# Scores of the 128-key tile in the burst and banks of the 384-key tile, and a VectorE write ahead of each burst

## The chip, the cores and the metric

The kernel runs on one core of one Trainium2 chip. The metric is device time in microseconds of one execution; the time before is the median of three runs, 1286.41 us (1285.4 to 1286.81). The profile is that of one further execution.

## The reference

Attention over 8 batches and 8 heads with 576 positions and 64 columns per head, masked in blocks of 64 (a query sees the keys of its own block and of those before it), and behind it a feed-forward network with a rational activation:

```python
scores = (1 / sqrt(64)) * q @ k^T                     # 8 x 8 heads, 576 x 576, float32
scores = where(block_i >= block_j, scores, -1e9)      # blocks of 64 positions
scores = scores - max(scores)
attn = exp(scores); attn = attn / (sum(attn) + 1e-9)
x = (attn @ v)                                        # put together to 4608 x 512
h = x @ w_in                                          # 512 -> 2048
P = a0 + a1*h + a2*h^2 + a3*h^3
Q = 1 + |b0|*|h| + |b1|*h^2
out = (P / (Q + 1e-6)) @ w_out                        # 2048 -> 512
```

## The kernel before

Attention runs over 32 pairs of heads (`NP`), two heads at a time: head 0 lies in partitions 0 to 63 of the prepared q and k, head 1 in 64 to 127. Matrix products are made of float32r parts: q and k are each split into a high and a low part, and three products (high-high, high-low, low-high) are added in PSUM.

A pair's queries are cut into five tiles, worked in the order `TILES = (4, 3, 2, 0, 1)`. Tile i below 4 has 128 queries and sees 128*(i+1) keys, so tile 3 is the 512-key tile, tile 2 the 384-key tile, tile 0 the 128-key tile, tile 1 the 256-key tile; tile 4 has the last 64 queries of both heads and 576 keys. Each tile is two steps (j = 0 and 1), so a pair has ten steps, and `attn_steps` hands out a list of what each step does: scores now, the exponential (`expo`) one step later, the transposes (`transp`) six steps later, and the products with v (`pv`) after that. `prep` of the next pair (transposes and splits of q and k) is put between.

For tiles 0 to 3 the scores of both heads are made at j = 0 in one burst. It takes two PSUM banks from a pool of five (`ps_a`, tag "a"), one for each head, and issues four matmuls for each head, in turn head 1 and head 0: first the mask (`MASKS[0]`; L504), a product of a constant row and column that puts a large negative number into the 64 columns that the first 64 queries must not see, and then the three score products (L507). These matmuls use 64 rows of the array each, and so two of them, one for each head, can run beside one another; nearly all other matmuls use all 128 rows. The helper `behind` fixes the order of a burst's matmuls among themselves, without a wait. At each step VectorE takes the maximum of one head's scores (`reduce_max`, L518; L514 for tile 4), and ACT makes the exponential from the bank with the maximum as bias (L529), which frees the bank.

The FFN runs over units of hidden columns: `first` (L210) makes h in one bank of its own, ACT, POOL and VectorE make the activation from it, and `second` (L277) multiplies with w_out. Attention steps from the fifth pair on emit a planned number of FFN half-steps, so FFN matmuls are the filler of the attention part; what is left of the FFN follows when attention is over.

The order of instructions on each engine is not written by hand: a scheduler plays the program through with a cost model when the kernel is built, and gives each engine its queue in the order in which things become ready there. On the chip each engine works its queue in that order and waits on semaphores. So a matmul whose bank is late in the plan can have other matmuls put ahead of it.

Names used below: PE is TensorE's matmul, PEld its weight load, DVE is VectorE, ACT ScalarE, POOL GpSimd. L567 are the transposes of the probabilities, whose results ACT copies (L580) and VectorE splits (L581); L594, L617 and L633 are products with v; L491 the scores of tile 4; L416 the transposes of `prep`.

Of the kernel before, what the change touches and what calls it, by code (L numbers as in the profile page):

```python
# [8 lines left out]
F32 = mybir.dt.float32  # L9
# [3 lines left out]
AF = mybir.ActivationFunctionType  # L13
ALU = mybir.AluOpType
AX = mybir.AxisListType
# [10 lines left out]
LEND = 4  # L26
RL = 3
C0 = 0
RW = 4
EV = 6  # L30
DP = 12
# [27 lines left out]
MASKS = ((None, None), (0, 0), (0, 1), (1, 0))  # L59
# [6 lines left out]
def attn_ffn_kernel(  # L66
# [11 lines left out]
    nc = tc.nc  # L78
# [30 lines left out]
    class Weights:  # L109
# [22 lines left out]
        def convert(self):  # L132
            last = []
            for key in self.places:
# [8 lines left out]
                                        in_=src.bitcast(I32).rearrange("(d p) f -> p d f", p=128))  # L143
                if there and len(last) >= RW:
                    tc.add_manual_dep(got.ins, last[-RW].ins.name,
                                      mybir.DependencyInfo(mybir.DependencyClass.Sync, mybir.DependencyReason.DATA),
# [26 lines left out]
    class Ffn:  # L173
# [8 lines left out]
        def load(self, ph, c):  # L182
            n = CTS[ph]
            nd = 512 // n
            self.x[ph, c] = []
            for i in range(4 // nd):

                pool = self.pools[-1] if ph and (4 * c + i) % 6 < 3 else ffn
                x = pool.tile([128, nd, 2, n], F32R, name=f"x{ph}_{c}_{i}", tag="x", bufs=XB)
                t0 = c * n  # L190
                while t0 < (c + 1) * n:
                    b = t0 // S
                    t1 = min((c + 1) * n, (b + 1) * S)
                    for d in range(nd):
                        nc.sync.dma_start(out=x[:, d, :, t0 - c * n:t1 - c * n].bitcast(F32),
                                          in_=xscr[b][:, nd * i + d, :, t0 - b * S:t1 - b * S])
                    t0 = t1
                self.x[ph, c] += [x[:, d] for d in range(nd)]
# [135 lines left out]
    with ExitStack() as actx:  # L334
        ps_a = actx.enter_context(tc.tile_pool(name="ps_a", bufs=5, space=PSUM))
# [9 lines left out]
        mrow = apers.tile([128, 128], F32R, name="mrow")  # L345
        mcol = apers.tile([128, 64], F32R, name="mcol")
# [55 lines left out]
        def behind(ins, first):  # L402
            tc.add_manual_dep(ins.ins, first.ins.name,
                              mybir.DependencyInfo(mybir.DependencyClass.NoSync, mybir.DependencyReason.DATA),
                              reason="order")
# [74 lines left out]
        def scores(p, d, j):  # L480
            s = st_[p]
            if j == 0:
                s[d] = tuple(att.tile([128, 2], F32, name=f"{n}{p}_{d}", tag=n, bufs=4) for n in ("nm", "sm"))
            nm, sm = s[d]
            i = TILES[d]
            q, k = s["q"], s["k"]
            if i == 4:
                c0, w = 288 * j, 288
                ps = ps_a.tile([128, 512], F32, name=f"s{p}_{d}_{j}", tag="a")
                for n, (x, y) in enumerate(((0, 0), (0, 1), (1, 0))):  # L490
                    nc.tensor.matmul(ps[:, :w], lhsT=qtl[p % 2][:, x], rhs=k[:, y, c0:c0 + w],  # L491
                                     start=(n == 0), stop=(n == 2))
                s[d, j] = ps
            else:
                w = 128 * (i + 1)
                if j == 0:
                    for h in range(2):
                        s[d, h] = ps_a.tile([128, 512], F32, name=f"s{p}_{d}_{h}", tag="a")
                    prev = None
                    for n, (x, y) in enumerate(MASKS):  # L500
                        for h in (1, 0):
                            hs = slice(64 * h, 64 * h + 64)
                            if x is None:
                                mm = nc.tensor.matmul(s[d, h][:, w - 64:w], lhsT=mrow[hs], rhs=mcol[hs],  # L504
                                                      start=(n == 0), stop=(n == 3), skip_group_check=(n == 0))
                            else:
                                mm = nc.tensor.matmul(s[d, h][:, :w], lhsT=q[hs, x, 128 * i:128 * i + 128],  # L507
                                                      rhs=k[hs, y, 0:w], start=(n == 0), stop=(n == 3),
                                                      skip_group_check=(MASKS[0][0] is None))
                            if prev is not None:  # L510
                                behind(mm, prev)
                            prev = mm
            if i == 4 and j == 1:
                nc.vector.tensor_tensor_reduce(out=trash, in0=s[d, j][:, :w], in1=zero.to_broadcast([128, 288]),  # L514
                                               scale=-1.0, scalar=nm[:, 0:1], op0=ALU.add, op1=ALU.min,
                                               accum_out=nm[:, 0:1])
            else:
                nc.vector.reduce_max(out=nm[:, j:j + 1], in_=s[d, j][:, :w], axis=AX.X, negate=True)  # L518

        def expo(p, d, j):  # L520
            s = st_[p]
            nm, sm = s[d]
            i = TILES[d]
            if i == 4 and j == 0:
                return
            for j2 in (0, 1) if i == 4 else (j,):
                n, w = (0, 288) if i == 4 else (j2, 128 * (i + 1))
                dst = pts[4][:, 288 * j2:288 * j2 + 288] if i == 4 else pts[i][:, j2]
                nc.scalar.activation(out=dst, in_=s.pop((d, j2))[:, :w], func=AF.Exp,  # L529
                                     bias=nm[:, n:n + 1], scale=1.0, accum_out=sm[:, j2:j2 + 1])  # L530
            if j == 0:
                return
            rc = att.tile([128, 2], F32, name=f"rc{p}_{d}", tag="rc", bufs=4)
            n = 1 if i == 4 else 2
            if i == 4:
                nc.gpsimd.tensor_tensor(out=sm[:, 0:1], in0=sm[:, 0:1], in1=sm[:, 1:2], op=ALU.add)
            nc.gpsimd.tensor_scalar_add(rc[:, :n], sm[:, :n], 1e-9)
            nc.vector.reciprocal(rc[:, :n], rc[:, :n])  # L538
            for j2 in range(n):
                x = pts[4][:, 0:S] if i == 4 else pts[i][:, j2]  # L540
                nc.gpsimd.tensor_scalar(out=x, in0=x, scalar1=rc[:, j2:j2 + 1], scalar2=1.0,  # L541
                                        op0=ALU.mult, op1=ALU.mult)
# [102 lines left out]
        def attn_steps():  # L645
# [8 lines left out]
            for k in range(len(items) + ALAG2 + ALAG3 + 8):  # L654
                for x in [x for x in todo if x[0] == k]:
                    todo.remove(x)
                    x[1](*x[2])
                if k < len(items):
                    p, d, j = items[k]
                    if (d, j) == (0, 0):  # L660
                        if p + 1 < NV:
                            o0, o1, o2 = OFFS
                            at(k + o0, load, p + 1)
                            at(k + o1, prep, p + 1, 0)
                            at(k + o2, prep, p + 1, 1)
                    at(k + ALAG2, expo, p, d, j)
                    if j == 1:
                        at(k + TLAG, transp, p, d)
                        if d == 4:
                            at(k + TLAG + 1, pv, p, 0)  # L670
                            at(k + TLAG + 2, pv, p, 1)
                            if p + 1 < NV:
                                at(k + TLAG + 2, vprep, p + 1)
                    scores(p, d, j)
                yield k
# [4 lines left out]
        load(0)  # L680
        for _ in range(C0):
            next(wsteps)
# [18 lines left out]
        NWA, NWB = 2 * NFA, 2 * NFB  # L701
        wdone = C0
        WSTEPS = [0] * C0 + [(W0 * (i + 1)) // 4 for i in range(4 - C0)] + [WA + WD * i // 4 for i in range(NWA - 4)]

# [56 lines left out]
```

## Time and profile before

| | |
|---|---|
| median of three runs | 1286.41 us |
| the profiled execution | 1287.04 us |
| its span from first to last instruction | 1285.3 us |
| mean granted TensorE clock | 0.998 |
| PE busy | 1255.0 us, 7644 matmuls |
| ACT busy | 925.3 us |
| DVE busy | 904.0 us |
| POOL busy | 880.5 us |
| DMA, mean | 120 GB/s |

The busy time of PE is a sum over spans whose ends are modelled: a matmul's row runs on while the next has begun. How fast work goes is therefore read from the distance between starts. In a timeline a row gives start, length, engine, line, operation, tiles and count; rows of one line that follow each other are merged. In a list of waits a row names who waited for whom, with the total in microseconds, the number of times and the longest. In the groups of instructions the numbers behind the bar are busy microseconds and the mean nanoseconds of one, and behind the next bar the idle time of the engine just before them and what ended it. The shares of the chain are shares of the time of the chain of work that ended last.

### The profile page before, as it was taken

To read this page: it belongs to the slowest core of one execution; us is meant where nothing else is said; L and a number is where in the kernel's file an instruction comes from. 1 tells how busy PE (TensorE), PEld (TensorE's weight loads), DVE (VectorE), ACT (ScalarE), POOL (GpSimd) and SP (SyncE) were. 2 spreads that over 40 slices of the span, in tenths; PEclk is the share of its full clock that TensorE was granted. 3 is DMA by queue.
4 is the path that set the end of the run, shared out by engine and by line. 5 is a ranking of instruction groups with operands and counts; after the bars stand their busy time and mean duration, and the time that the engine had idled before them with its cause. 6 is when DMAs were issued, how large, how long until landed. Compare 5 with 4: busy or idle time off the path is not lost.

```text
span 1285.3 us, 22748 instructions
## 1 busy us (share of the span) xinstructions
PE 1255.0 (98%) x7644; PEld 1059.5 (82%) x7644; DVE 904.0 (70%) x1703; ACT 925.3 (72%) x2047; POOL 880.5 (69%) x1041
## 2 busy tenths in 40 slices
PE   7989999999999999999999999999999999999997
PEld 5667888888888888888888888888998888888886
DVE  5767678777777777777767676754666767666675
ACT  5878777788678788777878787866766565555553
POOL 4656677777777878777767676766777666666564
PEclk9999999999999999999999999999999999999999
DMA  8772253445444354443432432356111433333423
GB/s 223 210 213 74 71 170 89 131 109 144 107 121 123 114 140 112 131 126 82 135 91 74 114 93 67 89 175 232 50 49 50 131 98 125 125 129 130 155 75 107
DMA packets 206516, 153.81 MB, mean 120 GB/s; under 512 B 137792, under 2 KB 170560, under 8 KB 206400
## 3 DMA queue, kind: packets, MB, share of 16 engines
q1 hardware_dynamic: 203920, 151.77, 40.5%
q8 instruction: 61, 1.00, 0.3%
q10 hardware_dynamic: 2416, 0.59, 0.2%
q14 instruction: 55, 0.45, 0.1%
q0 software_dynamic: 64, 0.00, 0.0%
HBM read 98.57 MB, written 44.04 MB: 111 GB/s over the span
## 4 chain that ended last, share of the span: by engine, by line
PE 82%; ACT 7%; DVE 4%; DMA 3%; POOL 3%; issue 1%; SPq 0%; ACTq 0%; POOLq 0%; DVEq 0%
PE h L210 30%; PE o L277 28%; PE o L633 6%; PE t L567 5%; PE s L507 4%; PE s L504 3%; ACT p L529 2%; PE tp L416 2%; PE s L491 1%; PE o L594 1%; DMA x<-xscr 1%; PE o L617 1%; DMA xscr<-xl 1%; POOL u L244 1%; ACT s L219 1%
## 5 line engine op out<-in xcount | busy, mean ns | idle before, releaser
L210 PE MATMUL h<-x,wpi 128*128 128x256 f32 (+1 forms) x2808 | 462.8, 312 | 3.1 <-DMA x<-xscr 1.7
L210 PEld LDWEIGHTS h<-x,wpi 128*128 128x128 f32 x2808 | 396.4, 190 | 40.6 <-issue 4.0
L277 PE MATMUL o<-wpo,gh 128*128 128x512 f32 x1152 | 351.0, 397 | 1.3 <-ACT os L287 1.3
L277 PEld LDWEIGHTS o<-wpo,gh 128*128 128x128 f32 x1152 | 211.1, 188 | 43.7 <-ACT os L287 1.8
L277 PE MATMUL o<-wpo,gl 128*128 128x512 f32 x576 | 213.8, 401 | 1.2 <-POOL gl L256 1.1
L224 POOL TENSOR_TENSOR u<-v,u 128x512 f32<-128x512 f32 x144 | 186.7, 1297 | 29.7 <-ACT v L220 24.6
L541 POOL TENSOR_SCALAR p<-p,rc 128x128 f32<-128x128 f32 (+4 forms) x288 | 169.2, 599 | 48.0 <-DVE rc L538 40.3
L529 ACT ACTIVATE p<-s,nm 128x288 f32<-128x288 f32 (+4 forms) x320 | 167.8, 533 | 45.1 <-DVE nm L518 39.9
L225 DVE TENSOR_TENSOR s<-s,h 128x512 f32<-128x512 f32 x144 | 98.4, 683 | 110.4 <-ACT s L219 56.7
L244 POOL TENSOR_TENSOR u<-s,u 128x512 f32<-128x512 f32 x90 | 116.7, 1297 | 72.1 <-DVE u L242 58.1
L232 ACT ACTIVATE v<-u,qcb 128x512 f32<-128x512 f32 x144 | 105.1, 730 | 74.7 <-POOL u L224 74.3
L217 ACT ACTIVATE u<-h 128x512 f32<-128x512 f32 x144 | 86.0, 597 | 93.7 <-PE h L210 87.9
L518 DVE TENSOR_REDUCE nm<-s 128x1 f32<-128x128 f32 (+4 forms) x288 | 128.5, 477 | 23.8 <-PE s L507 16.2
L567 PE MATMUL t<-ident,p 128*128 128x128 f32 x800 | 126.5, 281 | 0.9 <-POOL u L224 0.4
L581 DVE TENSOR_TENSOR ptrl<-t,ptrh 128x512 fp32r<-128x512 f32 (+1 forms) x182 | 111.6, 627 | 18.9 <-ACT ptrh L580 17.4
L277 PEld LDWEIGHTS o<-wpo,gl 128*128 128x128 f32 x576 | 104.3, 189 | 23.5 <-POOL gl L256 3.3
L256 POOL TENSOR_TENSOR gl<-u,v 128x512 fp32r<-128x512 f32 x90 | 118.6, 1317 | 3.4
L259 POOL TENSOR_TENSOR gl<-s,gh 128x512 fp32r<-128x512 f32 x54 | 69.9, 1294 | 62.9 <-ACT gh L258 62.9
L567 PEld LDWEIGHTS t<-ident,p 128*128 128x128 f32 x800 | 92.8, 142 | 23.1 <-issue 8.1
L580 ACT CAST ptrh<-t 128x512 fp32r<-128x512 f32 (+1 forms) x182 | 95.7, 545 | 18.8 <-PE t L567 18.2
L226 DVE SCALAR_TENSOR_TENSOR s<-s,coef,h 128x512 f32<-128x512 f32 x144 | 107.2, 744 | 2.9
L507 PE MATMUL s<-k,q 64*128 64x512 f32 (+3 forms) x768 | 103.5, 351 | 0.0
(109 smaller groups left out, 2105.6 us busy)
## 6 DMA issues: line engine op xcount, KB each, us to landing
x<-xscr SPq DMA_DIRECT2D x56, 256.0 KB, 3.8
xscr<-xl SPq DMA_DIRECT2D x32, 288.0 KB, 2.4
pscr<-os SPq DMA_DIRECT2D x18, 512.0 KB, 3.1
pt<-pscr SPq DMA_DIRECT2D x36, 256.0 KB, 4.3
out_dram<-os SPq DMA_DIRECT2D x36, 256.0 KB, 3.5
qr<-in_q_dram SPq DMA_DIRECT2D x64, 128.0 KB, 2.8
kr<-in_k_dram SPq DMA_DIRECT2D x62, 128.0 KB, 2.5
xt<-xh SPq DMA_DIRECT2D x52, 144.0 KB, 2.3
```

The source lines that it names most:

```text
L210: nc.tensor.matmul(h[:, j, :], lhsT=self.w[ph].win(f, dc, y), rhs=xs[dc][:, hl, :], start=(dc == 0 and i == 0), stop=(dc == 3 and i == 2))
L224: nc.gpsimd.tensor_tensor(out=ut, in0=vt, in1=ut, op=ALU.mult)
L226: nc.vector.scalar_tensor_tensor(out=st, in0=st, scalar=a1, in1=hf, op0=ALU.add if ph == 0 else ALU.subtract, op1=ALU.mult)
L244: nc.gpsimd.tensor_tensor(out=ut, in0=st, in1=ut, op=ALU.subtract)
L256: nc.gpsimd.tensor_tensor(out=gl, in0=ut, in1=vt, op=ALU.mult)
L277: nc.tensor.matmul(self.o[m], lhsT=g[:, j, ms], rhs=self.w[ph].wout(f, y), start=(u == 0 and j == 0 and i == 0), stop=(u == nu - 1 and j = ...
L507: mm = nc.tensor.matmul(s[d, h][:, :w], lhsT=q[hs, x, 128 * i:128 * i + 128], rhs=k[hs, y, 0:w], start=(n == 0), stop=(n == 3), skip_group ...
L518: nc.vector.reduce_max(out=nm[:, j:j + 1], in_=s[d, j][:, :w], axis=AX.X, negate=True)
L529: nc.scalar.activation(out=dst, in_=s.pop((d, j2))[:, :w], func=AF.Exp, bias=nm[:, n:n + 1], scale=1.0, accum_out=sm[:, j2:j2 + 1])
L541: nc.gpsimd.tensor_scalar(out=x, in0=x, scalar1=rc[:, j2:j2 + 1], scalar2=1.0, op0=ALU.mult, op1=ALU.mult)
L567: nc.tensor.transpose(ps[:, 128 * x:128 * x + 128], src[:, 128 * kb:128 * kb + 128], ident)
L581: nc.vector.tensor_tensor(out=dl, in0=src, in1=dh.bitcast(F32), op=ALU.subtract)
```

## The change

- The 128-key tile (i = 0) no longer takes banks and no longer has a burst of its own. Its scores are put into columns 384 to 511 of the 384-key tile's two banks, by three products for each head inside that tile's burst. One mask matmul for each head covers both tiles: its right-hand side is repeated, and it writes two groups of 64 columns (columns 320 to 383 and 448 to 511).
- Maximum and exponential of the 128-key tile stay at their own steps and read columns 384 to 511.
- Ahead of each burst (tiles 3, 2 and 1, with `TP = 0` for all pairs) VectorE writes 0.0 into column 0 of head 0's bank, which is the bank that the burst's second matmul writes. The burst's first matmul, which writes head 1's bank, waits for this write.

```diff
-                if j == 0:
-                    for h in range(2):
-                        s[d, h] = ps_a.tile([128, 512], F32, name=f"s{p}_{d}_{h}", tag="a")
+                if j == 0 and i:
+                    both = [ps_a.tile([128, 512], F32, name=f"s{p}_{d}_{h}", tag="a") for h in range(2)]
+                    parts = ((2, 0), (0, 384)) if i == 2 else ((i, 0),)
+                    for t, c in parts:
+                        for h in range(2):
+                            s["s", t, h] = both[h][:, c:c + 128 * (t + 1)]
                     prev = None
+                    held = nc.vector.memset(both[0][:, 0:1], 0.0) if p >= TP else None
                     for n, (x, y) in enumerate(MASKS):
-                        for h in (1, 0):
-                            hs = slice(64 * h, 64 * h + 64)
-                            if x is None:
-                                mm = nc.tensor.matmul(s[d, h][:, w - 64:w], lhsT=mrow[hs], rhs=mcol[hs],
-                                                      start=(n == 0), stop=(n == 3), skip_group_check=(n == 0))
-                            else:
-                                mm = nc.tensor.matmul(s[d, h][:, :w], lhsT=q[hs, x, 128 * i:128 * i + 128],
-                                                      rhs=k[hs, y, 0:w], start=(n == 0), stop=(n == 3),
-                                                      skip_group_check=(MASKS[0][0] is None))
-                            if prev is not None:
-                                behind(mm, prev)
-                            prev = mm
+                        for t, c in parts[:1] if x is None else parts:
+                            for h in (1, 0):
+                                hs = slice(64 * h, 64 * h + 64)
+                                if x is None:
+                                    m = both[h].rearrange("p (s t) -> p s t", t=64)[:, 2 * i + 1:8:2][:, :len(parts)]
+                                    mm = nc.tensor.matmul(m, lhsT=mrow[hs], start=True, stop=False, skip_group_check=True,
+                                                          rhs=mcol[hs].unsqueeze(1).to_broadcast([64, len(parts), 64]))
+                                else:
+                                    mm = nc.tensor.matmul(s["s", t, h], lhsT=q[hs, x, 128 * t:128 * t + 128],
+                                                          rhs=k[hs, y, 0:128 * (t + 1)], start=False, stop=(n == 3),
+                                                          skip_group_check=True)
+                                if prev is not None:
+                                    behind(mm, prev)
+                                elif held is not None:
+                                    tc.add_manual_dep(mm.ins, held.ins.name,
+                                                      mybir.DependencyInfo(mybir.DependencyClass.Sync, mybir.DependencyReason.DATA),
+                                                      reason="order")
+                                prev = mm
...
-                nc.vector.reduce_max(out=nm[:, j:j + 1], in_=s[d, j][:, :w], axis=AX.X, negate=True)
+                nc.vector.reduce_max(out=nm[:, j:j + 1], in_=s[d, j][:, :w] if i == 4 else s["s", i, j],
+                                     axis=AX.X, negate=True)
...
-                nc.scalar.activation(out=dst, in_=s.pop((d, j2))[:, :w], func=AF.Exp,
+                nc.scalar.activation(out=dst, in_=s.pop((d, j2))[:, :w] if i == 4 else s.pop(("s", i, j2)), func=AF.Exp,
                                      bias=nm[:, n:n + 1], scale=1.0, accum_out=sm[:, j2:j2 + 1])
```

More of the change, by code (lines that the diff above doesn't have):

```diff
@@ L28 @@
 C0 = 0
+TP = 0
 RW = 4
```

## The prediction

> **What bounds the kernel now.** I read the page's busy line first, then three stretches of the run, the chain of the middle stretch, TensorE's own waits there, and last the TensorE timeline around single bursts, because a busy line says nothing about the speed at which matmuls follow one another.
>
> ```profile
> PE 1255.0 (98%) x7644; PEld 1059.5 (82%) x7644; DVE 904.0 (70%) x1703; ACT 925.3 (72%) x2047; POOL 880.5 (69%) x1041
> ```
> ```profile
> 0.00:130.00 130.00, 115.73 (x679) 85.84 (x680) 90.23 (x214) 96.08 (x268) 74.92 (x140) 1.00 0.65 179
> 130.00:840.00 710.00, 703.32 (x4783) 603.53 (x4782) 526.08 (x1082) 563.19 (x1351) 526.47 (x664) 1.00 0.40 110
> 840.00:1285.00 445.00, 435.95 (x2186) 370.17 (x2184) 287.68 (x409) 266.03 (x430) 279.12 (x238) 1.00 0.36 117
> ```
> ```profile
> by line: PE h L210 23.6%; PE o L277 22.1%; PE o L633 10.3%; PE t L567 8.2%; PE s L507 6.3%; PE s L504 4.4%; PE tp L416 2.4%; PE s L491 1.9%; ACT p L529 1.9%; PE o L617 1.2%; issue 1.0%; POOL u L244 0.9%; ACT ptrh L580 0.9%; ACT s L219 0.8%;
> ```
>
> The columns of the second fence are the stretch, its length, busy time (and instructions) of PE, PEld, DVE, ACT and POOL, granted clock, DMA share and GB/s. The first 130 us are attention alone, up to 840 us attention runs with the FFN's first half as filler, and then only FFN is left; the change touches the first two. In the middle PE is busy 703 of 710 us at full clock, while ACT, the next, has 563. The third fence is the chain of that stretch by line: its nine PE lines add up to 80.4% (23.6 + 22.1 + 10.3 + 8.2 + 6.3 + 4.4 + 2.4 + 1.9 + 1.2). TensorE time taken out there should therefore come back at about 0.8 of its size. All waits of TensorE in that stretch:
>
> ```profile
> PE s L504 <- ACT p L529: 1.6, 2, 1.2
> PE o L277 <- POOL gl L256: 1.1, 3, 0.8
> PE o L633 <- ACT ptrh L580: 1.1, 1, 1.1
> PE o L617 <- ACT p L529: 0.7, 2, 0.5
> PE o L277 <- ACT os L287: 0.6, 1, 0.6
> PE h L210 <- DVE s L226: 0.5, 1, 0.5
> PE s L504 <- DVE ptrl L581: 0.5, 1, 0.5
> PE t L567 <- POOL u L224: 0.4, 1, 0.4
> ```
>
> Together 6.5 us (total, times, longest). So TensorE has something to do nearly always; what can be won is in how it does it.
>
> **What a burst costs.** A timeline row gives start and duration; the durations overlap, so I use starts. First a burst torn in two, then the spacing of undisturbed work (chain rows: start, length, work), then a 128-key burst in one piece.
>
> ```profile
> 402.73 0.28 PE L633 MATMUL o<-ptrl,vst 128*128 128x64 f32 x1
> 402.94 0.29 PE L504 MATMUL s<-mcol,mrow 64*128 64x64 f32 x1
> 403.16 0.97 PE L210 MATMUL h<-x,wpi 128*128 128x256 f32 x6
> 404.06 0.29 PE L504 MATMUL s<-mcol,mrow 64*128 64x64 f32 x1
> 404.06 0.66 PE L507 MATMUL s<-k,q 64*128 64x128 f32 x6
> ```
> ```profile
> 931.58 2.87 PE h L210 x24
> 442.00 0.44 PE t L567 x4
> ```
> ```profile
> 431.02 0.28 PE L633 MATMUL o<-ptrl,vst 128*128 128x64 f32 x1
> 431.23 0.30 PE L504 MATMUL s<-mcol,mrow 64*128 64x64 f32 x2
> 431.36 0.53 PE L507 MATMUL s<-k,q 64*128 64x128 f32 x6
> 431.82 0.50 PE L633 MATMUL o<-ptrh,vst 128*128 128x512 f32 x1
> 432.16 0.39 PE L633 MATMUL o<-ptrl,vst 128*128 128x512 f32 x1
> 432.39 0.37 PE L633 MATMUL o<-ptrh,vst 128*128 128x448 f32 x1
> 433.34 0.28 PE L633 MATMUL o<-ptrl,vst 128*128 128x64 f32 x1
> 433.45 0.65 PE L567 MATMUL t<-ident,p 128*128 128x128 f32 x4
> ```
>
> In the first, head 1's mask goes alone at 402.94, six FFN matmuls follow, and head 0's mask opens the rest at 404.06. From 402.73 that is 1.33 us. Without the lone mask: 0.11 from a 64-column L633 to the next full-height matmul (433.34 to 433.45), five FFN steps at 2.87/24 = 0.12, and 0.21 into the burst (431.02 to 431.23), together 0.92. A tear costs 0.41 us: TensorE goes twice more between 128-row and 64-row matmuls, and every passage shows 0.2 us instead of 0.1.
>
> The whole burst: 431.02 to 432.16 is 1.14 us, where L633 alone would take 0.11 + 0.23 (432.16 to 432.39) = 0.34. So it costs 0.80, of which three pairs of score matmuls at 0.11 (the 128-column spacing, 0.44/4) are work that stays; 0.47 is masks and the two passages.
>
> **The change part by part.**
>
> ```profile
> L504 PE MATMUL s<-mcol,mrow 64*128 64x64 f32 x256 | 62.0, 299 | 3.8 <-ACT p L529 2.3 <-ACT pt L578 0.9 <-DVE ptrl L581 0.5
> L507 PE MATMUL s<-k,q 64*128 64x128 f32 x192 | 19.3, 288 | 0.0
> 12.61 0.42 PE L504 MATMUL s<-mcol,mrow 64*128 64x64 f32 x1
> 834.03 0.29 PE L504 MATMUL s<-mcol,mrow 64*128 64x64 f32 x1
> L102 DVE MEMSET qcb<- 128x1 f32 x1 | 0.1, 59 | 0.8 <-PEq L745 0.8
> DVE s L225 <- ACT s L219: 26.8, 29, 2.4
> L581 DVE TENSOR_TENSOR ptrl<-t,ptrh 128x512 fp32r<-128x512 f32 (+1 forms) x182 | 111.6, 627 | 18.9 <-ACT ptrh L580 17.4
> ```
>
> - The 128-key tile's own burst goes, 32 times 0.47 = 15.0 us; 27 of them lie after 130 us (five stand in the timeline before): 12.7 us. 64 of the 256 masks and their weight loads go with it. Its three pairs of matmuls now stand in the 384-key burst, two steps earlier, and hide nothing and wait for nothing else: k and q are there.
> - The 384-key masks write 128 columns instead of 64. The rows give 299 ns for 64 columns of mask and 288 for 128 columns of scores: no difference; I take nothing (cover gone: 64 columns at half of 0.11, 32 times, 1.8 us).
> - Tears. The third and fourth rows are the first and the last of 73 lone masks, among 128 bursts; eight start before 130 us. The first matmul of a burst will now start only when its second bank is free too, so nothing is left to wait for between the two masks. 73 times 0.41 = 29.9 us, 65 of them, 26.7 us, after 130 us.
> - Banks: each pair takes two fewer of the five, and holds its 384-key banks two steps longer, until the 128-key exponentials. At the step of the 128-key scores that is two banks instead of three. Nothing taken.
> - VectorE gets 96 writes of one column (three bursts times 32 pairs) at 59 ns: 5.7 us on an engine with 184 us free of 710. No DMA and no POOL instruction moves.
> - The wait. TensorE stands at a burst until VectorE has come to the write; the whole TensorE queue stands behind it, the FFN filler too. VectorE's own queue stands if the bank is not yet free, behind it the score maxima, for which ACT's exponentials wait. No row has this wait. Low end: the two waits of TensorE on VectorE after 130 us, 1.0 us in all: 0.01 per burst. High end: VectorE waits 26.8/29 = 0.9 us for ACT in the last row but one above, is idle 26% of the stretch, and its mean instruction is 526/1082 = 0.49 us; a write arriving at any time finds half of what runs, 0.26 times 0.45 + 0.74 times 0.24 = 0.30 us, 29 us for 96. Below nothing it can't go, as the gain of the missing tears is counted already. The nearest row is the low one, a bank that VectorE frees and TensorE takes (L226), since the planned TensorE order puts the burst after the write; but nothing makes VectorE punctual, so I take 0.05, 5 us.
>
> The rule that speaks against it is in the Trainium skill, "TensorE: Matmul & The Clock Gate", Architectural detail: VectorE is a strict FIFO, and TensorE's window pulls only weight loads forward. By that rule nothing on either engine can pass the new wait, and the sum would be 1282, with the high end of the wait, against 1258 with mine. The present rows agree with TensorE waiting in order, but show it waiting on VectorE for only 1.0 us.
>
> Sum: after 130 us, 12.7 + 26.7 = 39.4 us of TensorE time, times 0.8 = 31.5. Before, 5 times 0.47 + 8 times 0.41 = 5.6 us, where TensorE is busy 116 of 130 us and much of the chain is DMA and ACT; I take 0.4, 2.3 us. Less the wait, 5: 29 us. The profiled execution took 1287.04 us (span 1285.3), 0.6 over the median of 1286.41; 1287 less 29 is 1258.
>
> **The rivals.**
> 1. *The tears stay or turn into waits.* The order only chains a burst's matmuls; filler may still be put between them. Or TensorE runs ahead of ACT, 79% busy after 130 us (563/710), and waits at banks instead. For it: the chain leaves TensorE for a fifth of the stretch. Against it: 6.5 us of TensorE waits. Then the burst's 12.7 times 0.8 = 10 us stay, less the wait 5, and a little of the tears, some 5: about 1277.
> 2. *VectorE sets the pace (the other side).* Each burst waits for one mean VectorE instruction more than planned, 0.49 us, 96 times: 47 us against 34: 1300. The place is the first mask of each burst; it decides from 34/96 = 0.35 us per burst on. For it: VectorE's in-order waits of 0.9 us, and the tears show that second banks come late. Against it: VectorE already has the last word on 182 banks of L581 alone (last row of that fence), and TensorE lost 1.0 us to VectorE after 130 us.
> 3. *High end of the wait.* 34 less 29 is 5 us: 1282.
>
> **How the numbers follow.** My forecast, 1242 to 1270, has 0.58 (1242: all 45 us come back; 1270: 0.55 of it and 0.08 us of wait per burst). Rival 1 has 0.12 and rival 3 has 0.07, together 1270 to 1284; no change 0.06; rival 2 0.17. Faster is thus 0.77, where 0.2% (2.6 us) is about what a measurement can tell from none. The range reaches from all of the gain to a small loss, 1241 to 1290; outside it are most of rival 2, and a little below. The forecast's own range is 1242 to 1270.
>
> **What would show it.** In the new profile: 192 masks instead of 256, in adjacent pairs, no lone one; 96 short VectorE writes; the middle stretch shorter by some 27 us with as much FFN in it, the last 445 us unchanged. A row of TensorE waiting on the new write shows the wait: under 10 us is my case, 30 us rival 3, over 34 us rival 2. Lone masks left, or new waits on ACT of 20 us, are rival 1. The prediction is wrong if a passage between 128-row and 64-row matmuls is not what the 0.2 us buy, that is, if filler next to whole bursts runs no faster than next to torn ones.

## The result: 1.2% faster, half of what was forecast

| | before | after |
|---|---|---|
| median of the runs compared | 1285.95 us | 1270.72 us |
| ratio (95% interval) | | 0.988 (0.9863 to 0.9897) |
| profiled execution | 1287.04 us | 1269.75 us |
| its span | 1285.3 us | 1267.9 us |
| PE busy | 1255.0 us | 1214.6 us |
| span less PE busy | 30.3 us | 53.3 us |

So 15.2 us came of a forecast 29. The time lies 0.7 us above the forecast's own stretch of 1242 to 1270, in the 1270 to 1284 that it gave to rivals 1 and 3, and inside its whole range of 1241 to 1290. The last two lines of the table already say what happened: TensorE's work shrank by 40.4 us, and its idle time grew by 23.0. The engines' busy line and the three stretches of the profile after, the second up to the end of attention (columns as before):

```profile
PE 1214.6 (96%) x7580; PEld 1037.2 (82%) x7580; DVE 908.5 (72%) x1799; ACT 923.7 (73%) x2047; POOL 882.3 (70%) x1041
```
```profile
0.00:130.00 130.00, 111.96 (x689) 83.12 (x689) 92.51 (x242) 100.48 (x276) 77.42 (x144) 0.96 0.65 181
130.00:832.00 702.00, 677.02 (x4780) 593.59 (x4778) 533.77 (x1160) 565.56 (x1357) 532.12 (x666) 1.00 0.41 112
832.00:1268.00 436.00, 425.59 (x2118) 360.50 (x2116) 282.21 (x398) 257.63 (x416) 272.72 (x232) 1.00 0.36 118
```

The same stretches of the kernel before, cut at the end of its attention:

```profile
130.00:851.00 721.00, 714.32 (x4855) 613.53 (x4853) 532.72 (x1093) 572.55 (x1367) 533.50 (x670) 1.00 0.40 109
851.00:1285.00 434.00, 424.95 (x2115) 360.17 (x2114) 281.03 (x398) 256.67 (x413) 272.09 (x231) 1.00 0.36 119
```

Nearly the same work (4855 less 75 matmuls, most of them the removed masks) took 702 us instead of 721. In it TensorE was idle for 721 - 714.3 = 6.7 us before and for 702 - 677.0 = 25.0 after. These 18.3 us are most of the 23.0; the first 130 us have 3.7 (18.0 us of idle time, 14.3 before). The FFN behind attention stayed at 434 and 436 us. One burst of the 384-key tile in the new TensorE timeline, and the instructions of the new write (durations are minimum, median and maximum; then the first and the last start):

```profile
415.76 0.33 PE L511 MATMUL s<-mcol,mrow 64*128 64x128 f32 x2
415.93 1.02 PE L514 MATMUL s<-k,q 64*128 64x384 f32 x12
416.88 0.66 PE L579 MATMUL t<-ident,p 128*128 128x128 f32 x4
L511 PE MATMUL s<-mcol,mrow x192: 264/295/419, 10.5 to 816.3; 64*128 64x64 f32 x128, 64*128 64x128 f32 x64
L504 DVE MEMSET s<- x96: 59/59/59, 9.1 to 810.9; 128x1 f32 x96
```

Both masks stand side by side, twelve score matmuls follow, and it is so in all 96 bursts: no lone mask is left of 73. The longest of TensorE's waits after 130 us:

```profile
PE o L278 <- POOL gl L257: 8.4, 9, 2.0
PE s L511 <- DVE ptrl L593: 2.5, 3, 1.3
PE t L579 <- DVE ptrl L593: 2.5, 3, 1.1
PE h L211 <- DVE s L227: 2.2, 4, 0.7
PE s L511 <- DVE s L504: 1.5, 1, 1.5
PE s L511 <- ACT p L541: 1.2, 4, 0.4
PE t L579 <- POOL u L245: 1.2, 1, 1.2
PE h L211 <- DMA x<-xscr: 1.0, 2, 0.6
PE t L579 <- POOL p L553: 1.0, 1, 1.0
```

The new write (L504) has 1.5 us of it (4.3 in the whole run). The largest is the FFN: the second product (L278, L277 before) waits 8.4 us for what POOL makes of the activation, against 1.1 before. With the small rows that are not shown, TensorE waits 10.6 us for POOL, 10.4 for VectorE and 2.7 for ACT, where it waited 1.5, 1.0 and 4.0 us before. So VectorE counts as much as POOL. In the chain of the stretch, too, other engines than TensorE take a larger part:

```profile
by line: PE h L211 18.6%; PE o L278 15.6%; PE o L645 7.9%; PE t L579 6.1%; PE s L514 4.5%; issue 3.4%; ACT p L541 2.9%; POOL gl L257 2.5%; POOL p L553 2.3%; DMA x<-xscr 1.9%; POOL u L245 1.8%; PE tp L417 1.7%; PE s L511 1.5%; PE s L492 1.4%
```

The TensorE lines shown add up to 57.3%, where those of the kernel before had 80.4%. (Both lists break off behind their longest entries.)

### The profile page after: what moved, and what is told of

The parts are those of the page before. It is cut to its first block, busy times and chain, and to the rows that moved or that the text cites. A ratio compares the mean times of both kernels' runs of the same rounds, so it can differ in the third digit from the quotient of the medians.

```text
span 1267.9 us, 22735 instructions
## 1 busy us (share of the span) xinstructions
PE 1214.6 (96%) x7580; PEld 1037.2 (82%) x7580; DVE 908.5 (72%) x1799; ACT 923.7 (73%) x2047; POOL 882.3 (70%) x1041
## 4 chain that ended last, share of the span: by engine, by line
PE 69%; ACT 9%; DVE 8%; POOL 6%; DMA 4%; issue 3%; SPq 1%; ACTq 0%; POOLq 0%; DVEq 0%
PE h L211 27%; PE o L278 25%; PE o L645 4%; PE t L579 4%; PE s L514 3%; ACT p L541 2%; PE o L606 2%; DMA x<-xscr 2%; POOL gl L257 1%; POOL p L553 1%; DVE nm L529 1%; PE tp L417 1%; POOL u L245 1%; PE s L511 1%; PE s L492 1%
## 5 line engine op out<-in xcount | busy, mean ns | idle before, releaser
L211 PE MATMUL h<-x,wpi 128*128 128x256 f32 (+1 forms) x2808 | 454.1, 310 | 6.4 <-DVE s L227 3.6
L211 PEld LDWEIGHTS h<-x,wpi 128*128 128x128 f32 x2808 | 393.9, 190 | 42.6 <-issue 5.3
L278 PE MATMUL o<-wpo,gh 128*128 128x512 f32 x1152 | 346.0, 395 | 1.5 <-ACT os L288 1.5
L278 PEld LDWEIGHTS o<-wpo,gh 128*128 128x128 f32 x1152 | 212.1, 189 | 43.9 <-ACT os L288 2.2
L278 PE MATMUL o<-wpo,gl 128*128 128x512 f32 x576 | 212.5, 401 | 8.5 <-POOL gl L257 8.4
L553 POOL TENSOR_SCALAR p<-p,rc 128x128 f32<-128x128 f32 (+4 forms) x288 | 174.2, 616 | 47.5 <-DVE rc L550 39.4
L529 DVE TENSOR_REDUCE nm<-s 128x1 f32<-128x128 f32 (+4 forms) x288 | 130.2, 479 | 17.7 <-PE s L514 10.1
L579 PE MATMUL t<-ident,p 128*128 128x128 f32 x800 | 123.7, 280 | 8.5 <-POOL p L553 4.3
L278 PEld LDWEIGHTS o<-wpo,gl 128*128 128x128 f32 x576 | 104.1, 189 | 32.8 <-POOL gl L257 13.1
L593 DVE TENSOR_TENSOR ptrl<-t,ptrh 128x512 fp32r<-128x512 f32 (+1 forms) x182 | 111.9, 629 | 15.2 <-ACT ptrh L592 14.2
L242 DVE TENSOR_TENSOR gh<-s,v 128x512 fp32r<-128x512 f32 x90 | 74.0, 822 | 47.0 <-ACT v L240 46.4
```

Of the source, the lines that this page charges most:

```text
L211: nc.tensor.matmul(h[:, j, :], lhsT=self.w[ph].win(f, dc, y), rhs=xs[dc][:, hl, :], start=(dc == 0 and i == 0), stop=(dc == 3 and i == 2))
L278: nc.tensor.matmul(self.o[m], lhsT=g[:, j, ms], rhs=self.w[ph].wout(f, y), start=(u == 0 and j == 0 and i == 0), stop=(u == nu - 1 and j = ...
L529: nc.vector.reduce_max(out=nm[:, j:j + 1], in_=s[d, j][:, :w] if i == 4 else s["s", i, j], axis=AX.X, negate=True)
L579: nc.tensor.transpose(ps[:, 128 * x:128 * x + 128], src[:, 128 * kb:128 * kb + 128], ident)
L593: nc.vector.tensor_tensor(out=dl, in0=src, in1=dh.bitcast(F32), op=ALU.subtract)
```

## The experiments

Theory 1: TensorE's saving is real, and half of it returned because POOL, ACT and VectorE could not follow. Theory 2: the wait on VectorE gave it back. Each edit changes what the scheduler plans, so the order of all engines differs a little between any two of these kernels. Besides medians I therefore compare profiled executions in three parts: TensorE busy, span less busy (idle), and the start of the last product with v, which ends attention: 850.8 us before, 832.0 after. "The seam" below is where attention ends and only FFN is left.

**The halves of the change, and the wait by itself.** The merge alone:

```diff
-TP = 0
+TP = 99
```

> The 128-key tile shares burst and banks of the 384-key tile, but no VectorE write and no wait (TP = 99). 56 of 96 bursts are still torn in the TensorE order (73 of 128 before). Theory 1 (TensorE's saving is real, and about half of it comes back as waits for POOL, ACT and VectorE, which can't follow a faster TensorE): 15 us of bursts and 7 of tears saved, half of it returned: about 1275. Theory 2 (the wait on VectorE gave the gain back): without the wait nothing is given back, 0.8 of 22 us: about 1268, no slower than the whole change.

Measured 1288.98 us, ratio 1.0019 (1.0008 to 1.0029): no gain, outside both. TensorE is busy for 1242.5 us, 12.5 less where 22 had been expected, and idle for 45.7, 15.4 more. Attention ends at 845.7, 5.1 earlier, and what follows takes 442.5 us instead of 434.5. There, from 835 to 910 us, TensorE waits:

```profile
PE o L278 <- POOL gl L257: 5.9, 2, 3.6
PE h L211 <- DMA x<-xscr: 2.1, 1, 2.1
PE h L211 <- DVE s L227: 1.8, 1, 1.8
```

I read this as one FFN unit at the seam that has nothing beside it to cover its latency; no run changes the seam alone. It is a second term, of some 8 us, that an edit in attention can switch. It is half of the idle time gained: another 5.4 us lie in the first 130 us (19.7 us idle, 14.3 before).

The hold alone, on the kernel before, ahead of all 128 bursts:

```diff
                     prev = None
+                    held = nc.vector.memset(s[d, 0][:, 0:1], 0.0)
...
                             if prev is not None:
                                 behind(mm, prev)
+                            else:
+                                tc.add_manual_dep(mm.ins, held.ins.name,
+                                                  mybir.DependencyInfo(mybir.DependencyClass.Sync, mybir.DependencyReason.DATA),
+                                                  reason="order")
```

> The kernel before with the VectorE write and the wait ahead of all 128 bursts, the 128-key tile in a burst of its own. No torn burst. Theory 1: 30 us of tears saved, half returned: about 1271 to 1274. Theory 2: 24 us won, some 20 given back by the wait: about 1282.

Measured 1282.9 us, 0.9966 (0.9953 to 0.998), where theory 2 had put it. But among TensorE's waits after 130 us, the write (L500) ends little. The three longest, and the row of burst openings that names it:

```profile
PE s L505 <- DVE ptrl L586: 4.5, 3, 2.1
PE s L505 <- ACT p L534: 3.7, 5, 1.5
PE o L277 <- POOL gl L256: 2.3, 5, 0.8
PE s L505 <- DVE s L500: 1.1, 1, 1.1
```

The first two are waits of burst openings (L505) for banks that VectorE and ACT still read. TensorE is busy for 1228.5 us, 26.5 less, and idle for 52.8, 22.5 more; of these 8.1 lie in the first 130 us (22.4 us idle, 14.3 before).

The whole change without the wait; the write stays:

```diff
-                                elif held is not None:
-                                    tc.add_manual_dep(mm.ins, held.ins.name, ...)
```

> The whole change with the VectorE write, but the burst's first matmul does not wait for it (the second, into the written bank, does). 5 of 96 bursts are torn in the TensorE order. Theory 1: as the whole change, 1268 to 1273. Theory 2: the wait's price is gone, 1255 to 1260.

Measured 1271.17 us, 0.9881 (0.9867 to 0.9895): the whole change's time. The explicit wait costs nothing that can be measured; it mends the last 5 torn bursts, which doesn't show in the time either. The burst's second matmul still waits for the write here, so this run alone does not clear the write; but TensorE waits for it 2.0 us in all here and 4.3 in the whole change, and there the write had ended 3.1 us before its burst opened (median of the 96). Against 23.0 us of new idle time theory 2 falls. What mended nearly all tears is the write itself. With it only 5 of 96 bursts are torn; without it, in the merge alone, 56. A plausible reason is that the write claims head 0's bank ahead of the first mask, so that the first mask gets the later of the two; the order shows the effect, not the reason. The chain of this kernel from 130 to 833 us, for a comparison further down:

```profile
by line: PE h L211 15.2%; PE o L278 13.1%; PE o L641 6.9%; PE t L575 4.9%; issue 4.8%; ACT p L537 3.8%; PE s L514 3.4%; POOL gl L257 3.3%; POOL p L549 2.9%; POOL u L245 2.6%; DVE gh L242 1.9%; DMA x<-xscr 1.9%; POOL u L225 1.8%; DVE ptrl L5
```

Merged, without write and wait, but with masks over all 128 rows:

```diff
-TP = 0
+TP = 99
...
-mm = nc.tensor.matmul(m, lhsT=mrow[hs], ...
-                      rhs=mcol[hs].unsqueeze(1).to_broadcast([64, len(parts), 64]))
+mm = nc.tensor.matmul(m, lhsT=mrow, ...
+                      rhs=mcol.unsqueeze(1).to_broadcast([128, len(parts), 64]))
```

> Merged tiles, no VectorE write, and the mask matmuls use all 128 rows (both constant rows, so the masked columns get twice the large negative number). Torn bursts stay in the order (56 of 96), but a lone mask is no passage between 128-row and 64-row matmuls any more and should cost 0.11 us and not 0.41. TensorE work saved: about 40 us less some 9 for masks that no longer run in pairs. Theory 1: half of 31 comes back, about 1270. Theory 2: no wait on VectorE, 0.8 of 31: about 1261.

Measured 1285.09 us, 0.9991 (0.9981 to 1.0002), outside both. TensorE's busy time fell by 22.8 us where 31 had been expected, and idle time rose by 25.7; attention ended at 845.5, and the rest took 442.7 us, the seam of the merge alone again. The seam is some 8 of the 25.7 us. The mean granted clock of this profiled execution was 0.979, against 0.998 before, so what a lone mask of 128 rows costs cannot be read from these sums.

**Is POOL where the gain went?** The same division on POOL left out of both kernels:

```diff
-            for j2 in range(n):
-                x = pts[4][:, 0:S] if i == 4 else pts[i][:, j2]
-                nc.gpsimd.tensor_scalar(out=x, in0=x, scalar1=rc[:, j2:j2 + 1], scalar2=1.0,
-                                        op0=ALU.mult, op1=ALU.mult)
```

> The kernel before, leaving out the division of the probabilities by their sums on POOL (L541, 288 instructions, 169 us of POOL). It is the base for the next kernel. If TensorE alone sets the pace before, as its 6.5 us of waits after 130 us say, little changes: 1275 to 1287.

> The whole change, leaving out the same division on POOL. Theory 1 (the gain comes back because POOL, and what hangs on it, can't follow a faster TensorE): with 169 us less on POOL the distance to the kernel before with the same part left out grows from 15 to 25 to 35 us. Rival (the new waits come from the order and the banks, whatever POOL's load): the distance stays at 12 to 18 us.

Measured 1299.05 us (1.0096, 1.0079 to 1.0112) and 1257.9 us (0.9774, 0.9759 to 0.9789). The distance is 41 us, beyond the 25 to 35 of theory 1; but the base, expected at 1275 to 1287, moved the wrong way, 12 us slower with less work. Some of the 41 is the seam (434.7 us behind attention against 441.3). By the end of attention alone it is 855.4 against 821.9, 33.5 us, where it was 18.8. Of the 14.7 us between, 10.1 are the changed kernel's, whose attention ended earlier, and 4.6 the old kernel's, whose attention ended later. The stretches from 130 us to there, first the kernel before without the division, then the changed one:

```profile
130.00:855.00 725.00, 720.31 (x4898) 618.49 (x4897) 531.30 (x1104) 577.19 (x1386) 398.20 (x445) 1.00 0.40 109
130.00:822.00 692.00, 680.90 (x4841) 598.55 (x4837) 527.36 (x1175) 571.78 (x1376) 398.46 (x442) 1.00 0.42 114
```

TensorE idles 4.7 and 11.1 us here. POOL's relief took the changed kernel's idle time from 25.0 to 11.1 us and left the old kernel's nearly alone (6.7 to 4.7). TensorE's waits for VectorE fell with those for POOL (10.4 to 3.3 and 10.6 to 4.5 us). The edit takes away POOL's load and also a step between the exponential and the transposes; it doesn't separate the two. In the changed kernel the wait for POOL's `gl` fell from 8.4 to:

```profile
PE o L278 <- POOL gl L257: 4.5, 7, 1.7
```

The hold alone with the same part left out:

> The hold alone (128 bursts, the 128-key tile in its own), leaving out the division on POOL. The hold alone saved 22.7 us of TensorE time in attention and only 2.0 us of its length. Theory 1 (POOL gave it back): against the kernel before with the same part left out (1299) 0.8 of 22.7 comes through: 1275 to 1283. Rival (the second pair of banks of the 128-key tile is what holds the bursts up; merged, it is not needed): 1290 to 1299.

Measured 1281.8 us (0.9966, 0.9952 to 0.998), in theory 1's interval: 17 us less than its base, where the hold alone had won 3.6. Attention ends at 843.5, 11.9 earlier than 855.4 (2.0 earlier with the division in). But 4.6 us of the 9.9 between are again the base's own later end; the hold's attention ended 5.3 us earlier without the division. So POOL probably took part of this gain too, not all: burst openings still wait 5.4 us for ACT's exponentials and 4.0 for VectorE.

A smaller relief:

```diff
-            nc.gpsimd.tensor_scalar_add(rc[:, :n], sm[:, :n], 1e-9)
-            nc.vector.reciprocal(rc[:, :n], rc[:, :n])
+            nc.vector.reciprocal(rc[:, :n], sm[:, :n])
```

> The whole change, and VectorE takes the reciprocal of the sums as they are; the 160 additions of 1e-9 on POOL (40 us) and one passage from POOL to VectorE are gone (a sum is at least 1, so the addition changes no bit). Theory 1 (POOL's pace takes part of the gain): 5 to 10 us faster than the whole change, 1261 to 1266. Rival (waits from the order alone): 1268 to 1273.

> The kernel before with the same 160 additions gone. 64 of 128 bursts torn in the TensorE order instead of 73. Theory 1: TensorE sets the pace and POOL's 40 us are off the path, so only the tears count, 1281 to 1287. Rival (POOL's chain already counted before): as much faster as in the changed kernel, 1276 to 1281.

Measured 1269.46 us (0.987, 0.9854 to 0.9886) and 1295.74 us (1.0064, 1.0052 to 1.0076). The first is the whole change's time, not better, and in the rival's interval: attention ended at 824.9, 7.1 earlier, and TensorE's idle time from 130 us to there fell from 25.0 to 14.6, but the rest took 441.3 us instead of 435.9. The second is outside both ranges, 9 us slower with less work. Twice now the old kernel lost when POOL had less to do. I did not settle why; its plan changed, TensorE was idle for 40.6 us instead of 30.3, and the waits are spread over many pairs. So an edit that only takes work away left the old kernel with 7.0 us more idle time between 130 us and the end of attention (6.7 to 13.7). The 10.4 and 13.9 us that the two reliefs took from the changed kernel are more than that, but not by far: that POOL's chain took back part of the gain is likely, and how much is open.

**The price of a passage.** 160 lone matmuls in the changed kernel, with 64 rows, and with 128 (`[0:64]` left out):

```diff
                 ps = bank(p, f"t{p}_{d}_{gi}")
...
+                if gi == 0:
+                    nc.tensor.matmul(ps[:, 0:64], lhsT=mrow[0:64], rhs=mcol[0:64], start=True, stop=True, skip_group_check=True)
```

> The whole change with 160 more lone mask matmuls of 64 rows, one ahead of the first transposes of each tile, into columns that the transposes then overwrite. If a passage between 128-row and 64-row matmuls is what costs, each adds 0.4 us of TensorE work, 0.3 more than one of 128 rows: 24 to 48 us more than the next kernel, 1300 to 1330. If it is not: the same as the next kernel within 3 us.

> The same 160 lone matmuls with 128 rows, so no passage: 160 times 0.11 = 18 us of TensorE work, part of it in TensorE's waits: 1275 to 1289.

Measured 1297.81 us (1.0081, 1.0062 to 1.01) and 1285.57 us (0.9987, 0.9973 to 1.0). The timelines, first 64 rows, then 128:

```profile
399.79 0.40 PE L211 MATMUL h<-x,wpi 128*128 128x256 f32 x2
400.11 0.29 PE L578 MATMUL t<-mcol,mrow 64*128 64x64 f32 x1
400.34 0.66 PE L581 MATMUL t<-ident,p 128*128 128x128 f32 x4
```
```profile
394.00 0.19 PE L578 MATMUL t<-mcol,mrow 128*128 128x64 f32 x1
394.03 0.65 PE L581 MATMUL t<-ident,p 128*128 128x128 f32 x4
```

The transposes start 0.23 us behind the one and 0.03 behind the other. Over the 34 places between an L211 and a transpose, the three distances from the L211 to the second transpose have medians of 0.209, 0.225 and 0.165 us against 0.120, 0.030 and 0.156: 0.29 us for a passage out and back, as the expectation had it (0.3). The Trainium skill ("TensorEngine Tiling (Array Packing)", Key Properties) says that changing the tiling mode drains TensorE, without a figure; these distances agree with that. TensorE is busy for 1252.8 against 1228.7 us. But the time differs by 12.2 us, half the lower end expected: 45 of the 160 stood beside a burst's matmuls, which have 64 rows too, and so added no passage, and idle time took some of the rest (44.2 us against 53.6).

**Banks.**

```diff
-ps_a = actx.enter_context(tc.tile_pool(name="ps_a", bufs=5, space=PSUM))
+ps_a = actx.enter_context(tc.tile_pool(name="ps_a", bufs=4, space=PSUM))
```

> The whole change with four banks in the attention pool instead of five. If banks are what the two bursts of the 384-key and the 128-key tile fight for, and the merge helps by needing two fewer, one bank less costs as much as the merge won, 12 us and more: over 1282. If banks are not short, below 1274.

Measured 1343.79 us, 1.0433 (1.0414 to 1.0452). TensorE is busy for 1243.1 of 1340.1 us. So banks are scarce even after the merge. That fits the merge and the hold winning 5.1 and 2.0 us of attention apart and 18.8 together; the two banks saved may be the reason, but this run takes one away for every user and doesn't show it.

## Why the prediction was right, and where its size came from

- *What a burst and a tear cost.* Right. The work saved was put at 45 us; TensorE's busy time fell by 40.4. Its two terms can be read apart where no burst is torn: the hold alone took 26.5 us off (29.9 forecast for the tears), and from there to the whole change it is another 13.9 (15.0 forecast for the burst). The passage measured by itself has 0.29 us.
- *The tears go.* Right: 73 to none. The reason was wrong in a detail: the write does nearly all of it, and the wait only the last 5.
- *The wait, 5 us (0.01 to 0.30 per burst).* Its own row has 4.3 us in all, and taking it out changes nothing. Rivals 2 and 3 did not happen: most bursts opened well after their write had ended. The strict FIFO of VectorE that the Trainium skill states ("TensorE: Matmul & The Clock Gate", Architectural detail) makes such a wait possible; 4.3 us over 96 bursts is what it came to here.
- *39.4 us of TensorE time, "times 0.8".* This is the term that was mis-sized. Attention ended 18.8 us earlier, 0.47 of 40. The 0.8 was the share of TensorE in the chain of the kernel before; TensorE then waited for other engines, 18.3 us more after 130 us, and its share fell to 57%. The share doesn't measure how much comes through: in the kernel without the explicit wait, which took the same time, the TensorE lines shown above add up to 43.5%. The forecast's rival 1 had this in its second half ("or TensorE runs ahead ... and waits"), but named ACT. The waits that grew were for POOL, 74% busy before (526 of 710 us), and VectorE, also 74% busy (526), less than ACT's 79%. So how busy an engine is did not tell who would be waited for.
- *The range.* The time fell inside it because it also had room for half of the gain; the forecast's own stretch, which reached down to 0.55 of the gain with a dearer wait, was missed by 0.7 us. That the mechanism was right is the forecast's merit; that the number still fell in the whole range is owed to its width.
- *The last part unchanged.* Right here (434 and 436 us), by luck: several variants lost 5 us and more at the seam, which the forecast did not price.
- *Banks, "nothing taken".* Open. One bank less costs 73 us, so banks are short; whether that is why the two halves of the change do not add up, no run shows.

## What to carry to other kernels

The share of an engine in the chain is not the rate at which saved time comes back: here it was 0.8, and of TensorE's saved work 0.47 came through with the whole change, 0.4 with the merge alone (5.1 of 12.5 us) and less than 0.1 with the hold alone (2.0 of 26.5), by the end of attention. So discount such a saving by the chains that will be waited for next. Matmuls of half the rows should come in whole bursts, since each lone one costs a passage there and back (0.29 us here); a write ahead of a burst can be enough to keep it together in the planned order (56 torn bursts to 5 here). Under a planned order every edit moves the order everywhere, so read the stage that was edited and the seams behind it apart before two variants are compared by their total.

## What had not been expected

- A one-column write of 59 ns on VectorE took the planned order from 56 torn bursts to 5, without a wait of the burst's first matmul for it.
- Removing POOL work made the old kernel slower, by 12 and by 9 us.
- The granted TensorE clock dipped more in kernels with more idle time: 0.92 and 0.96 in the first 130 us of the kernels without division and of the changed one, against 1.00 before. What the dips cost was not measured. They lengthen matmuls, and so stand in TensorE's busy time and not in its idle time: in the changed kernel six score matmuls of 512 keys from 408.89 us on took 1.33 us, with the clock at 0.50 from 409.3 to 412.7, and the same six took 0.93 at 417.87 before. By the mean clocks of the two profiled executions (0.998 and 0.993 over 1268 us) I estimate that they hide at most some 6 us of the work saved.
